# Transposing bf16 data as fp32 pairs in a channel-attention and mixture-of-adapters kernel

## The chip, the cores and the metric

The kernel runs on one core of a Trainium2 chip. The metric is the device time of one execution in microseconds. The kernel before takes 255.24 us (median of 2 runs, 255.1 to 255.38). Its profile covers a span of 253.5 us.

## The reference

For each of four batches, q and k (6400 rows by 256 channels) are normalised along the rows. Their 256 by 256 channel product goes through a softmax, and v is multiplied by it. On each row of the result, a gate picks two of eight experts by its logits; each expert is a rank-16 adapter, and its output is added to the row.

```python
qn = q / (np.linalg.norm(q, axis=1, keepdims=True) + 1e-06)
kn = k / (np.linalg.norm(k, axis=1, keepdims=True) + 1e-06)
a = softmax(kn.transpose(0, 2, 1) @ qn / tau)          # 256 x 256, per batch
x = v @ a                                              # 25600 x 256
# logits = x @ w_gate; two largest of 8 -> weights w
# out = x + sum over the two experts e of  w_e * (x @ A[e]) @ B[e]
```

## The kernel before

A planner orders all steps ahead of time and fixes the engine of each. Four steps matter here. `do_G` builds the channel product on TensorE with k as the stationary operand. `do_T` transposes v on TensorE, 128 x 128 bf16 at a time, into PSUM; `do_Te` copies the result to SBUF on ScalarE or VectorE ("eviction"). The gated product `gz` is formed on VectorE, transposed on TensorE (`do_gzT`) and evicted. `do_Y` multiplies the transposed v by the softmax and the transposed gated product by the adapters' B. Between them, matmuls with the transposed v as weights give logits and adapter inputs (`do_ZL`, `do_log`, `do_Z`).

```python
# cut: constants P = 128, CC = 2 channel halves, C = 256, E = 8, ER = 128; a unit u has n = 4 or 2 columns
    def do_G(s, b, c):
        if c == 0:
            st[b]["acc"] = [psum.tile([P, 512], FP32, tag=f"acc{ic}", name=f"acc{ic}") for ic in range(CC)]
        acc = st[b]["acc"]
        (qt, j), (kt, _) = qk_of("q", b, c), qk_of("k", b, c)
        for ic in range(CC):
            nc.tensor.matmul(
                acc[ic][:, 0:256], kt[:, j, ic * P:(ic + 1) * P], qt[:, j, :],
                start=c == 0, stop=False, skip_group_check=True)
# cut: k against itself and q against itself, for the norms:
        for ic in range(0 if (b, group_of(c), "k") in OFF else CC):
            nc.tensor.matmul(
                acc[ic][:, 256:384], kt[:, j, ic * P:(ic + 1) * P],
                kt[:, j, ic * P:(ic + 1) * P],
                start=False, stop=False, skip_group_check=True)
# cut
    def do_T(s, b, i, u):
        c, n = UNITS[u]
        g = max(g for g, (i0, _) in enumerate(V) if i0 <= i)
        vt = held["v", (b, g), ""][:, (i - V[g][0]) * PC:, :]
        sb(s, "vT", (b, i), [P, CC, PC, P], BF16)
        ps = bank(s, ("T", b, i, u), [P, CC, n, P], BF16)
        for ic in range(CC):
            for j in range(n):
                nc.tensor.matmul(
                    ps[:, ic, j, :], vt[:, c + j, ic * P:(ic + 1) * P], W["ident"],
                    is_transpose=True, start=(ic + j == 0), stop=(ic == CC - 1 and j == n - 1))

    def do_Te(s, b, i, u):
        c, n = UNITS[u]
        copy(s, held["vT", (b, i), ""][:, :, c:c + n, :], held["bank", ("T", b, i, u)])
# cut
    def do_Ze(s, b, i, u):
        c, n = UNITS[u]
        gz = sb(s, "gz", (b, i, u), [P, n, ER], BF16)
        z = held["zl", (b, i), ""][:, c:c + n, E:] if (b, i) in MERGED else held["bank", ("Z", b, i, u)]
        nc.vector.tensor_tensor(
            out=gz.rearrange("p c (e r) -> p c e r", e=E),
            in0=z.rearrange("p c (e r) -> p c e r", e=E),
            in1=held["gate", (b, i), "g2"][:, c:c + n, :].to_broadcast([P, n, E, R]), op=OP.mult)
# cut
    def do_gzT(s, b, i, u):
        c, n = UNITS[u]
        gz = held["gz", (b, i, u), ""]
        sb(s, "gzT", (b, i, u), [P, n, P], BF16)
        ps = bank(s, ("gzT", b, i, u), [P, n, P], BF16)
        for j in range(n):
            nc.tensor.matmul(ps[:, j, :], gz[:, j, :], W["ident"], is_transpose=True,
                             start=(j == 0), stop=(j == n - 1))
# cut
    def do_Y(s, b, i, c):
        u = unit_of(c)
        vT, gzT = held["vT", (b, i), ""], held["gzT", (b, i, u), ""]
        ps = bank(s, ("Y", b, i, c), [P, 2, C], FP32)
        for j in range(2):
            for ic in range(CC):
                nc.tensor.matmul(
                    ps[:, j, :], vT[:, ic, c + j, :], st[b]["a"][:, ic, :],
                    start=(j == 0 and ic == 0), stop=False, skip_group_check=True)
        for j in range(2):
            nc.tensor.matmul(ps[:, j, :], gzT[:, c + j - UNITS[u][0], :], W["B"],
                             start=False, stop=(j == 1), skip_group_check=True)
```

## Time and profile before

| | before |
|---|---|
| time, median | 255.24 us |
| busy TensorE / VectorE / ScalarE | 215.6 / 190.1 / 167.6 us |
| bf16 transposes of v and of gz | 400 and 200 |
| HBM read and written | 78.9 and 26.2 MB, 415 GB/s over the span |
| last TensorE matmul, last eviction, end of span | 245.4, 246.0, 253.5 us |

These lines are from the profile's page of the kernel before: busy time of each engine, then the granted TensorE clock and the busy share of the DMA engines in tenths over 40 slices, then groups of instructions. A group shows line, engine and operation, tile written and read, shapes and count, then busy us and the mean ns of one instruction, then idle time before it and who ended that.

```profile
PE 215.6 (85%) x2643; PEld 192.3 (76%) x2643; DVE 190.1 (75%) x486; ACT 167.6 (66%) x270; POOL 29.9 (12%) x58
...
PEclk9999897699999999999999999999999999999996
DMA  9999999999999999999999999999999999999994
...
L750 ACT COPY vT<-T_ps 128x1024 bf16<-128x1024 bf16 (+1 forms) x44 | 37.0, 871 | 6.7 <-PE T_ps L770 6.5
...
L770 PE MATMUL T_ps<-ident,v 128*128 128x128 bf16 x400 | 26.8, 219 | 0.8 <-DMA v<-in_v_dram 0.8
...
L870 DVE TENSOR_TENSOR gz<-zl,gateg 128x512 bf16<-128x512 f32 (+1 forms) x42 | 23.5, 597 | 0.3
...
L881 PE MATMUL gzT_ps<-ident,gz 128*128 128x128 bf16 x200 | 19.7, 219 | 0.3
```

DMA is busy for nine tenths or more of nearly every slice. A bf16 transpose has a record of 219 ns, but the records overlap, so that is a latency (from start to end of one) and not a cost (the time for which it keeps the engine from the next). The cost is read from the chain of waits, which gives start, length and count of each piece of a stream:

```profile
137.56 0.44 PE Y_ps L894 x4
137.99 0.22 PE Y_ps L898 x2
138.21 1.12 PE T_ps L770 x20
139.33 0.22 PE acc L575 x2
139.54 0.11 PE acc L579 x2
```

Twenty transposes take 1.12 us: 56 ns each. Two 256-column matmuls take 0.22 us (109 ns each) and two 128-column ones 0.11 us (56 ns).

The last view before the change gives busy us in stretches of the span: columns as in the header, then the granted clock, the DMA share and GB/s.

```profile
core 0: us, PE busy (x) PEld busy (x) DVE busy (x) ACT busy (x) POOL busy (x), PEclk, DMA share, GB/s
230.00:240.00 10.00, 10.00 (x132) 9.27 (x131) 8.66 (x25) 7.82 (x15) 0.00 (x0) 1.00 1.01 423
244.00:246.00 2.00, 1.40 (x13) 1.01 (x11) 0.00 (x0) 1.79 (x4) 0.00 (x0) 1.00 1.00 408
246.00:248.00 2.00, 0.00 (x0) 0.00 (x0) 0.00 (x0) 0.02 (x1) 0.00 (x0) 1.00 1.02 414
248.00:250.00 2.00, 0.00 (x0) 0.00 (x0) 0.00 (x0) 0.00 (x0) 0.00 (x0) 0.92 0.74 297
```

### The profile page before, as it was taken

How to read it: one execution, taken by the hardware profiler on the slowest of the kernel's cores; microseconds unless marked ns; L12 is line 12 of the kernel's file. 1: busy time of each engine (PE TensorE's matmuls, PEld its weight loads, DVE VectorE, ACT ScalarE, POOL GpSimd, SP SyncE). 2: the span in 40 equal slices, each digit the busy share in tenths (PEclk: the TensorE clock that was granted, in tenths of full speed). 3: DMA queues.
4: the chain of work that ended last, by engine and by line, in shares of the span. 5: the costliest groups of instructions: out<-in, count | busy, mean ns of one | idle time of the engine just before them, and what ended most of it. 6: DMA issues, size and time to landing. Idle time of an engine off the chain costs nothing.

```text
span 253.5 us, 6344 instructions
## 1 busy us (share of the span) xinstructions
PE 215.6 (85%) x2643; PEld 192.3 (76%) x2643; DVE 190.1 (75%) x486; ACT 167.6 (66%) x270; POOL 29.9 (12%) x58
## 2 busy tenths in 40 slices
PE   1173993899999999999989999979999979999970
PEld 0051982688999996799779999779999869989860
DVE  0055589779889978898979995689888888888910
ACT  4354437558786767888758768453877869768770
POOL 7001220040020002000030100510000210000000
PEclk9999897699999999999999999999999999999996
DMA  9999999999999999999999999999999999999994
GB/s 223 211 215 212 212 217 213 213 216 216 218 215 211 318 295 293 259 214 219 209 216 221 217 216 217 210 211 345 284 278 323 331 322 319 316 421 427 427 411 196
DMA packets 11820, 66.60 MB, mean 263 GB/s; under 512 B 1424, under 2 KB 2320, under 8 KB 7184
## 3 DMA queue, kind: packets, MB, share of 16 engines
q0 software_dynamic: 7488, 38.93, 74.8%
q1 hardware_dynamic: 3968, 26.74, 26.0%
q10 hardware_dynamic: 336, 0.53, 0.6%
q8 instruction: 20, 0.33, 0.5%
q14 instruction: 8, 0.07, 0.1%
HBM read 78.91 MB, written 26.21 MB: 415 GB/s over the span
## 4 chain that ended last, share of the span: by engine, by line
PE 49%; DMA 39%; ACT 3%; DVE 3%; POOL 2%; issue 1%; ACTq 0%; POOLq 0%
DMA qk<-in_k_dram 22%; PE Y_ps L894 13%; DMA v<-in_v_dram 9%; DMA qk<-in_q_dram 8%; PE acc L575 7%; PE Y_ps L898 6%; PE T_ps L770 6%; PE ZL_ps L792 4%; PE gzT_ps L881 3%; PE acc L584 2%; PE acc L579 2%; PE Z_ps L861 2%; DVE a_bf L744 2%; ACT a_exp L696 1%; PE log_ps L807 1%
## 5 line engine op out<-in xcount | busy, mean ns | idle before, releaser
L575 PE MATMUL acc<-qk 128*128 128x256 bf16 x400 | 70.6, 286 | 20.1 <-DMA qk<-in_k_dram 14.0
L603 DVE TENSOR_TENSOR ssq<-ssq,sq 128x1280 f32<-128x1280 f32 (+1 forms) x27 | 43.4, 1607 | 26.8 <-ACT sq L597 24.8
L894 PE MATMUL Y_ps<-a_bf,vT 128*128 128x256 bf16 x400 | 60.0, 273 | 0.0
L597 ACT ACTIVATE sq<-qk 128x1280 f32<-128x1280 bf16 (+1 forms) x27 | 36.8, 1364 | 26.2 <-DVE ssq L603 19.7
L750 ACT COPY y<-Y_ps 128x512 f32<-128x512 f32 x79 | 45.7, 587 | 12.4 <-PE Y_ps L898 9.8
L575 PEld LDWEIGHTS <-qk 128*128 128x128 bf16 x400 | 33.7, 102 | 24.4 <-DMA qk<-in_k_dram 16.0
L750 ACT COPY vT<-T_ps 128x1024 bf16<-128x1024 bf16 (+1 forms) x44 | 37.0, 871 | 6.7 <-PE T_ps L770 6.5
L894 PEld LDWEIGHTS <-vT 128*128 128x128 bf16 x400 | 37.6, 98 | 3.7
L898 PE MATMUL Y_ps<-ball,gzT 128*128 128x256 bf16 x200 | 38.2, 273 | 0.3 <-DVE gzT L752 0.3
L579 PE MATMUL acc<-qk 128*128 128x128 bf16 x242 | 34.0, 223 | 0.0
L770 PE MATMUL T_ps<-ident,v 128*128 128x128 bf16 x400 | 26.8, 219 | 0.8 <-DMA v<-in_v_dram 0.8
L560 POOL DMA_DIRECT2D v<-in_v_dram x20 | 12.2, 609 | 126.9 <-PE T_ps L770 80.7
L579 PEld LDWEIGHTS <-qk 128*128 128x128 bf16 x242 | 24.4, 101 | 3.5
L770 PEld LDWEIGHTS <-v 128*128 128x128 bf16 x400 | 23.7, 98 | 1.7 <-DMA v<-in_v_dram 1.4
L870 DVE TENSOR_TENSOR gz<-zl,gateg 128x512 bf16<-128x512 f32 (+1 forms) x42 | 23.5, 597 | 0.3
L584 PE MATMUL acc<-qk 128*128 128x128 bf16 x168 | 23.5, 222 | 0.0
L898 PEld LDWEIGHTS <-gzT 128*128 128x128 bf16 x200 | 19.4, 98 | 3.0 <-DVE gzT L752 0.6
L792 PE MATMUL ZL_ps<-waA_sb,vT 128*128 128x136 bf16 x280 | 19.6, 222 | 1.1 <-DVE waA_sb L738 0.9
L881 PE MATMUL gzT_ps<-ident,gz 128*128 128x128 bf16 x200 | 19.7, 219 | 0.3
L752 DVE COPY gzT<-gzT_ps 128x512 bf16<-128x512 bf16 (+1 forms) x39 | 15.0, 390 | 5.6 <-PE gzT_ps L881 4.8
L792 PEld LDWEIGHTS <-vT 128*128 128x128 bf16 x280 | 17.7, 98 | 1.8 <-issue 1.5
L597 ACT ACTIVATE ssq<-qk 128x1536 f32<-128x1536 bf16 x8 | 11.9, 1483 | 9.7 <-DMA qk<-in_q_dram 5.1
(79 smaller groups left out, 273.8 us busy)
## 6 DMA issues: line engine op xcount, KB each, us to landing
out_dram<-y SPq DMA_DIRECT2D x18, 1280.0 KB, 17.9
v<-in_v_dram POOLq DMA_DIRECT2D x20, 640.0 KB, 20.5
qk<-in_q_dram POOLq DMA_DIRECT2D x7, 1088.0 KB, 24.1
qk<-in_k_dram POOLq DMA_DIRECT2D x7, 1088.0 KB, 28.8
qk<-in_q_dram POOLq DMA_DIRECT2D x2, 1024.0 KB, 18.7
qk<-in_k_dram POOLq DMA_DIRECT2D x2, 1024.0 KB, 23.1
out_dram<-y SPq DMA_DIRECT2D x4, 512.0 KB, 7.0
qk<-in_q_dram POOLq DMA_DIRECT2D x2, 512.0 KB, 17.1
```

Of the source, the lines that this page charges most:

```text
L575: nc.tensor.matmul(acc[ic][:, 0:256], kt[:, j, ic * P:(ic + 1) * P], qt[:, j, :], start=c == 0, stop=False, skip_group_check=True)
L579: nc.tensor.matmul(acc[ic][:, 256:384], kt[:, j, ic * P:(ic + 1) * P], kt[:, j, ic * P:(ic + 1) * P], start=False, stop=False, skip_group_ ...
L584: nc.tensor.matmul(acc[ic][:, 384:512], qt[:, j, ic * P:(ic + 1) * P], qt[:, j, ic * P:(ic + 1) * P], start=False, stop=c == NC - 1, skip_ ...
L597: nc.scalar.activation(out[:, 0:n, :], t[:, j:j + n, :], ACT.Square)
L603: nc.vector.tensor_tensor(out=t, in0=t, in1=held["sq", (w, b, g), ""][:, 0:n, :], op=OP.add)
L750: nc.scalar.copy(out, in_)
L770: nc.tensor.matmul(ps[:, ic, j, :], vt[:, c + j, ic * P:(ic + 1) * P], W["ident"], is_transpose=True, start=(ic + j == 0), stop=(ic == CC ...
L792: nc.tensor.matmul(ps[:, j, :], vT[:, ic, c + j, :], st[b]["waA"][:, ic, :], start=(j == 0 and ic == 0), stop=(j == n - 1 and ic == CC - 1 ...
L870: nc.vector.tensor_tensor(out=gz.rearrange("p c (e r) -> p c e r", e=E), in0=z.rearrange("p c (e r) -> p c e r", e=E), in1=held["gate", (b ...
L881: nc.tensor.matmul(ps[:, j, :], gz[:, j, :], W["ident"], is_transpose=True, start=(j == 0), stop=(j == n - 1))
L894: nc.tensor.matmul(ps[:, j, :], vT[:, ic, c + j, :], st[b]["a"][:, ic, :], start=(j == 0 and ic == 0), stop=False, skip_group_check=True)
L898: nc.tensor.matmul(ps[:, j, :], gzT[:, c + j - UNITS[u][0], :], W["B"], start=False, stop=(j == 1), skip_group_check=True)
```

## The change

The intent is to halve the transposes. Two neighbouring bf16 values are taken as one fp32 value, so that one 128 x 128 fp32 transpose moves what two bf16 transposes moved. After it, each partition holds a pair of even and odd channel, so the weights taken from the transposed v are read at every second bf16, and k's channels are taken with stride 2 to match. For the gated product the pair is two neighbouring rows. VectorE must therefore write gz interleaved, which it does with one instruction for every two columns in place of one for the unit.

```diff
         ident = const.tile([P, P], BF16, name="ident")
         make_identity(nc, ident)
         W["ident"] = ident
+        W["ident32"] = const.tile([P, P], FP32, name="ident32")
+        nc.vector.tensor_copy(W["ident32"], ident)
 # cut; the channel product, k with stride 2 (also in the row-norm sums of k):
             nc.tensor.matmul(
-                acc[ic][:, 0:256], kt[:, j, ic * P:(ic + 1) * P], qt[:, j, :],
+                acc[ic][:, 0:256], kt[:, j, ic::CC], qt[:, j, :],
                 start=c == 0, stop=False, skip_group_check=True)
         for ic in range(0 if (b, group_of(c), "k") in OFF else CC):
             nc.tensor.matmul(
-                acc[ic][:, 256:384], kt[:, j, ic * P:(ic + 1) * P],
-                kt[:, j, ic * P:(ic + 1) * P],
+                acc[ic][:, 256:384], kt[:, j, ic::CC],
+                kt[:, j, ic::CC],
                 start=False, stop=False, skip_group_check=True)
         for ic in range(0 if (b, group_of(c), "q") in OFF else CC):
             nc.tensor.matmul(
 # cut; transposes of v, and how their result is read:
-        sb(s, "vT", (b, i), [P, CC, PC, P], BF16)
-        ps = bank(s, ("T", b, i, u), [P, CC, n, P], BF16)
-        for ic in range(CC):
-            for j in range(n):
-                nc.tensor.matmul(
-                    ps[:, ic, j, :], vt[:, c + j, ic * P:(ic + 1) * P], W["ident"],
-                    is_transpose=True, start=(ic + j == 0), stop=(ic == CC - 1 and j == n - 1))
+        sb(s, "vT", (b, i), [P, PC, P], FP32)
+        ps = bank(s, ("T", b, i, u), [P, n, P], FP32)
+        for j in range(n):
+            nc.tensor.matmul(ps[:, j, :], vt[:, c + j, :].bitcast(FP32), W["ident32"],
+                             is_transpose=True, start=(j == 0), stop=(j == n - 1))
 
     def do_Te(s, b, i, u):
         c, n = UNITS[u]
-        copy(s, held["vT", (b, i), ""][:, :, c:c + n, :], held["bank", ("T", b, i, u)])
+        copy(s, held["vT", (b, i), ""][:, c:c + n, :], held["bank", ("T", b, i, u)])
+
+    def vT_of(b, i, c):
+
+        return held["vT", (b, i), ""][:, c, :].bitcast(BF16).rearrange("p (t cc) -> p t cc", cc=CC)
 # cut; the same in do_log and do_Z:
-                    ps[:, j, :], vT[:, ic, c + j, :], st[b]["waA"][:, ic, :],
+                    ps[:, j, :], vT_of(b, i, c + j)[:, :, ic], st[b]["waA"][:, ic, :],
 # cut; the gated product and its transposes:
-        nc.vector.tensor_tensor(
-            out=gz.rearrange("p c (e r) -> p c e r", e=E),
-            in0=z.rearrange("p c (e r) -> p c e r", e=E),
-            in1=held["gate", (b, i), "g2"][:, c:c + n, :].to_broadcast([P, n, E, R]), op=OP.mult)
+        pairs = gz.rearrange("p c d -> p (c d)").rearrange("p (h x two) -> p h two x", two=2, x=ER)
+        for h in range(n // 2):
+            nc.vector.tensor_tensor(
+                out=pairs[:, h].rearrange("p c (e r) -> p c e r", e=E),
+                in0=z[:, 2 * h:2 * h + 2, :].rearrange("p c (e r) -> p c e r", e=E),
+                in1=held["gate", (b, i), "g2"][:, c + 2 * h:c + 2 * h + 2, :].to_broadcast([P, 2, E, R]), op=OP.mult)
 
     def do_gzT(s, b, i, u):
         c, n = UNITS[u]
         gz = held["gz", (b, i, u), ""]
-        sb(s, "gzT", (b, i, u), [P, n, P], BF16)
-        ps = bank(s, ("gzT", b, i, u), [P, n, P], BF16)
-        for j in range(n):
-            nc.tensor.matmul(ps[:, j, :], gz[:, j, :], W["ident"], is_transpose=True,
-                             start=(j == 0), stop=(j == n - 1))
+        sb(s, "gzT", (b, i, u), [P, n // 2, P], FP32)
+        ps = bank(s, ("gzT", b, i, u), [P, n // 2, P], FP32)
+        pairs = gz.rearrange("p c d -> p (c d)").bitcast(FP32)
+        for j in range(n // 2):
+            nc.tensor.matmul(ps[:, j, :], pairs[:, j * P:(j + 1) * P], W["ident32"], is_transpose=True,
+                             start=(j == 0), stop=(j == n // 2 - 1))
 # cut; do_Y:
-                    ps[:, j, :], vT[:, ic, c + j, :], st[b]["a"][:, ic, :],
+                    ps[:, j, :], vT_of(b, i, c + j)[:, :, ic], st[b]["a"][:, ic, :],
                     start=(j == 0 and ic == 0), stop=False, skip_group_check=True)
         for j in range(2):
-            nc.tensor.matmul(ps[:, j, :], gzT[:, c + j - UNITS[u][0], :], W["B"],
+            pair = gzT[:, (c - UNITS[u][0]) // 2, :].bitcast(BF16).rearrange("p (t two) -> p t two", two=2)
+            nc.tensor.matmul(ps[:, j, :], pair[:, :, j], W["B"],
                              start=False, stop=(j == 1), skip_group_check=True)
 
```

The tile of zeros for warm-up matmuls is halved and read twice, to make room for the fp32 identity.

More of the change, by code (lines that the diff above doesn't have):

```diff
@@ L507, in make_consts @@
         W["neg"] = neg
-        W["zeros"] = const.tile([P, 512], BF16, name="zeros")
+        W["zeros"] = const.tile([P, 256], BF16, name="zeros")
         nc.vector.memset(W["zeros"], 0.0)
@@ L616, in do_n2p @@
         for ic in range(CC):
-            nc.tensor.matmul(ps[:, ic:ic + 1], st[b]["ssq" + w][:, ic * P:(ic + 1) * P],
+            half = slice(ic, None, CC) if w == "k" else slice(ic * P, (ic + 1) * P)
+            nc.tensor.matmul(ps[:, ic:ic + 1], st[b]["ssq" + w][:, half],
                              W["ones"][:, 0:1], start=(ic == 0), stop=(ic == CC - 1),
@@ L757, in do_warm @@
     def do_warm(s, n):
-        nc.tensor.matmul(bank(s, ("warm", n), [P, 512], FP32), W["ident"], W["zeros"],
+        nc.tensor.matmul(bank(s, ("warm", n), [P, 512], FP32), W["ident"], W["zeros"][:, None, :].to_broadcast([P, 2, 256]),
                          start=True, stop=True)
@@ L786, in do_ZL @@
         c, n = ZUNITS[z]
-        vT = held["vT", (b, i), ""]
         sb(s, "zl", (b, i), [P, PC, E + ER], FP32)
@@ L801, in do_log @@
     def do_log(s, b, i):
-        vT = held["vT", (b, i), ""]
         gate_tiles(s, b, i)
@@ L807, in do_log @@
                 nc.tensor.matmul(
-                    ps[:, j, :], vT[:, ic, j, :], st[b]["awg"][:, ic, :],
+                    ps[:, j, :], vT_of(b, i, j)[:, :, ic], st[b]["awg"][:, ic, :],
                     start=(j == 0 and ic == 0), stop=(j == PC - 1 and ic == CC - 1),
@@ L855, in do_Z @@
         c, n = UNITS[u]
-        vT = held["vT", (b, i), ""]
         sb(s, "gz", (b, i, u), [P, n, ER], BF16)
@@ L861, in do_Z @@
                 nc.tensor.matmul(
-                    ps[:, j, :], vT[:, ic, c + j, :], st[b]["aA"][:, ic, :],
+                    ps[:, j, :], vT_of(b, i, c + j)[:, :, ic], st[b]["aA"][:, ic, :],
                     start=(j == 0 and ic == 0), stop=(j == n - 1 and ic == CC - 1),
@@ L889, in do_Y @@
         u = unit_of(c)
-        vT, gzT = held["vT", (b, i), ""], held["gzT", (b, i, u), ""]
+        gzT = held["gzT", (b, i, u), ""]
         ps = bank(s, ("Y", b, i, c), [P, 2, C], FP32)
```

## The prediction

> **What bounds it now.** Two things at once. The page's slices show DMA at 9 tenths in all but the last; HBM moves 415 GB/s; the windows view has a DMA share of 0.95 to 1.08 in every 10 us up to 250. That traffic is untouched. From about 52 us on TensorE is full too: 9.4 to 10.0 us busy per 10 us nearly everywhere, and the chain of waits is TensorE without a break from 208 to 245 us, then one eviction and the last store (to 253.5). VectorE is busy 75%, ScalarE 66%.
>
> **What the change does.**
>
> 1. TensorE, transposes: 400 + 200 bf16 become 200 + 100 fp32. A bf16 one costs 56 ns in a stream (20 in 1.12 us in the chain), a pair 112. No fp32 transpose is in the trace. Its fp32 matmuls: with one column, four records take 0.42 us, so an fp32 weight load takes about 105 ns, against at most 24 to 28 for bf16 (8-column logit matmuls); with 256 columns a pass takes about 240 ns, double the bf16 109. The Trainium skill, "TensorE: Matmul & The Clock Gate", Weight-path perf modes, says fast weight load needs a non-FP32 dtype; the trace agrees. Every fp32 instruction here leaves two records (two passes), but the page's Terms call transpose mode 4x faster for FP32, which I take as one pass; no run shows it. Then an fp32 transpose is bound by its weight load, 105 to 120 ns (estimate), equal to the pair it replaces: 300 x (-7 to +8 ns) = -2 to +2 us. With two passes, 210 to 240 ns: +30 to +38 us.
> 2. TensorE, stride 2: k weights, moving k, and all weights from vT and gzT read every second bf16. "SBUF — State Buffer", cachelines note: stride is free up to 8 bf16. No instruction of before shows it; I expect intervals of 109, 59 and 56 ns unchanged. Without fast load, 128- and 136-column matmuls would go from 56-59 to about 105 ns.
> 3. ScalarE: vT evictions 1015 to about 590 ns (29), 593 to 385 (15), gzT 585 to 385 (12): -19 us busy.
> 4. VectorE: its bf16 evictions were already fast (684 ns for 1024 bf16, 690 for 512 fp32): no gain. The gate product splits: 40 of 687 ns become 80 of about 416, +6 us busy, and each transpose starts 0.15 us later.
>
> The order of steps on each engine stays; transposes merge.
>
> **On the critical path.** ScalarE's 19 us are not (late in the span it waits mostly for TensorE). Of VectorE's 6 us perhaps 1. The TensorE terms are, from 52 us on, and cancel to within 2 us. The DMA floor forbids much gain: a TensorE saving of 15 us would show 2 to 4.
>
> **Predicted: 256.0 us, range 252.5 to 277.** Faster by over 2%: 0.03; within 2%: 0.66; slower by over 2%: 0.31. The high side carries two passes and lost fast load.
>
> **What would show it.** 200 and 100 transpose records, ten in about 1.1 us (twice the records or 2 us: step 1 wrong). Intervals of Y 109, merged logit 59, k Gram 56 ns: step 2 right. ScalarE busy near 149 us, VectorE near 196. DMA at 9 tenths throughout, last y eviction at 245 to 247 us.
>
> **What would make it wrong.** Two passes; transpose-mode loads that cannot be prefetched behind a running matmul; strided weights without fast load (+20 us or more); fp32 transposes that let the granted clock fall below 1.0 after 60 us; VectorE, near 0.9 busy in mid-span, pushed over by the split product.

## More of the kernel before

The timeline shows two transposes of gz between 256-column matmuls of Y, with TensorE's weight loads (PEld) beside them. Columns are start, length, engine and instruction:

```profile
239.22 0.21 PEld L881 LDWEIGHTS <-gz 128*128 128x128 bf16 x2
239.33 0.28 PE L881 MATMUL gzT_ps<-ident,gz 128*128 128x128 bf16 x2
...
239.44 0.38 PE L894 MATMUL Y_ps<-a_bf,vT 128*128 128x256 bf16 x2
```

From the start of the first transpose (239.33) to the start of the next matmul (239.44) TensorE gives 0.11 us to the pair.

TensorE looks full from 230 to 240 us, with DMA full beside it. After TensorE has ended, DMA goes on at 414 GB/s for two more microseconds and is not idle before 250.

## The result, and the profile after

| | before | after |
|---|---|---|
| time, median of 2 runs | 255.24 us | 255.25 us (255.21 to 255.28) |
| busy TensorE / VectorE / ScalarE | 215.6 / 190.1 / 167.6 | 218.9 / 193.2 / 150.0 us |
| transposes of v and of gz | 400 and 200 bf16 | 200 and 100 fp32 |
| span | 253.5 us | 253.4 us |

The ratio is 0.9995, 95% interval 0.9971 to 1.0019: the same. Ratios with an interval are not quite the ratio of the quoted medians.

The page after, the same groups:

```profile
PE 218.9 (86%) x2343; PEld 193.1 (76%) x2343; DVE 193.2 (76%) x527; ACT 150.0 (59%) x270; POOL 29.9 (12%) x58
...
PEclk9999996599999999999999999999999999999996
DMA  8999999999999999999999999999999999999995
...
L772 PE MATMUL T_ps<-ident,v 128*128 128x128 f32 x200 | 27.8, 281 | 0.6 <-DMA v<-in_v_dram 0.6
...
L753 ACT COPY vT<-T_ps 128x512 f32<-128x512 f32 (+1 forms) x44 | 21.7, 516 | 9.2 <-PE T_ps L772 8.8
...
L874 DVE TENSOR_TENSOR gz<-zl,gateg 128x256 bf16<-128x256 f32 x70 | 26.0, 444 | 0.3
...
L886 PE MATMUL gzT_ps<-ident,gz 128*128 128x128 f32 x100 | 20.4, 278 | 0.0
```

There is one record for each fp32 transpose, 200 and 100, and not two. ScalarE's evictions of v fell from 37.0 to 21.7 us. VectorE's largest group of gz rose from 23.5 to 26.0 us; that line leaves out the products read straight from PSUM, which went from 10.6 to 11.4 us. TensorE's busy time rose by 3.3 us although the intervals below show no more work: it counts all time covered by a record, and a record (281 and 278 ns for an fp32 transpose) lasts longer than the engine is held. The intervals in the chain of waits say what was paid:

```profile
137.41 0.11 PE Y_ps L904
137.52 1.09 PE T_ps L772 x10
138.61 0.22 PE acc L577 x2
138.83 0.11 PE acc L581 x2
```

Ten fp32 transposes take 1.09 us, 109 ns each, for what took 112 ns as two bf16 ones. The channel product, now with k at stride 2 both as weights (L577) and as the moving operand (L581), still takes 0.22 and 0.11 us for two. The timeline around one lone fp32 transpose of gz:

```profile
239.21 0.38 PE L904 MATMUL Y_ps<-ball,gzT 128*128 128x256 bf16 x2
...
239.32 0.14 PEld L886 LDWEIGHTS gzT_ps<-ident,gz 128*128 128x128 f32 x1
239.42 0.27 PE L886 MATMUL gzT_ps<-ident,gz 128*128 128x128 f32 x1
239.43 0.21 PEld L899 LDWEIGHTS <-vT 128*128 128x128 bf16 x2
239.53 0.27 PE L899 MATMUL Y_ps<-a_bf,vT 128*128 128x256 bf16 x1
```

Its weight load starts at 239.32, while the matmuls of B are still running, and the transpose still holds TensorE from 239.42 to 239.53: 0.11 us, as the pair of bf16 ones did at the same place. The last stretches:

```profile
core 0: us, PE busy (x) PEld busy (x) DVE busy (x) ACT busy (x) POOL busy (x), PEclk, DMA share, GB/s
230.00:240.00 10.00, 10.00 (x112) 9.29 (x111) 8.97 (x30) 6.99 (x15) 0.00 (x0) 1.00 1.01 425
244.00:246.00 2.00, 1.48 (x14) 1.08 (x11) 0.00 (x0) 1.79 (x4) 0.00 (x0) 1.00 1.01 413
246.00:248.00 2.00, 0.00 (x0) 0.00 (x0) 0.00 (x0) 0.11 (x1) 0.00 (x0) 1.00 1.03 415
248.00:250.00 2.00, 0.00 (x0) 0.00 (x0) 0.00 (x0) 0.00 (x0) 0.00 (x0) 0.67 0.77 309
```

DMA has the same shares in the same places.

### The profile page after: what moved, and what is told of

Read it like the earlier page. It is cut to its first block, busy times and chain, and to the rows that moved or that the text cites. A ratio compares the mean times of both kernels' runs of the same rounds, so it can differ in the third digit from the quotient of the medians.

```text
span 253.4 us, 5843 instructions
## 1 busy us (share of the span) xinstructions
PE 218.9 (86%) x2343; PEld 193.1 (76%) x2343; DVE 193.2 (76%) x527; ACT 150.0 (59%) x270; POOL 29.9 (12%) x58
## 4 chain that ended last, share of the span: by engine, by line
PE 49%; DMA 42%; DVE 2%; ACT 2%; POOL 1%; issue 1%; ACTq 0%; POOLq 0%
DMA qk<-in_k_dram 28%; PE Y_ps L899 12%; PE acc L577 9%; DMA qk<-in_q_dram 8%; PE T_ps L772 6%; PE Y_ps L904 6%; DMA v<-in_v_dram 6%; PE ZL_ps L796 4%; PE gzT_ps L886 4%; PE acc L586 2%; PE acc L581 2%; PE Z_ps L863 2%; PE log_ps L810 1%; DVE a_bf L747 1%; POOL qk L562 1%
## 5 line engine op out<-in xcount | busy, mean ns | idle before, releaser
L577 PE MATMUL acc<-qk 128*128 128x256 bf16 x400 | 71.2, 285 | 17.5 <-DMA qk<-in_k_dram 10.7
L577 PEld LDWEIGHTS <-qk 128*128 128x128 bf16 x400 | 34.7, 103 | 22.7 <-DMA qk<-in_k_dram 13.6
L899 PEld LDWEIGHTS <-vT 128*128 128x128 bf16 x400 | 38.9, 98 | 4.0
L581 PE MATMUL acc<-qk 128*128 128x128 bf16 x242 | 34.4, 224 | 0.0
L772 PE MATMUL T_ps<-ident,v 128*128 128x128 f32 x200 | 27.8, 281 | 0.6 <-DMA v<-in_v_dram 0.6
L753 ACT COPY vT<-T_ps 128x512 f32<-128x512 f32 (+1 forms) x44 | 21.7, 516 | 9.2 <-PE T_ps L772 8.8
L581 PEld LDWEIGHTS <-qk 128*128 128x128 bf16 x242 | 24.3, 100 | 3.4
L874 DVE TENSOR_TENSOR gz<-zl,gateg 128x256 bf16<-128x256 f32 x70 | 26.0, 444 | 0.3
L772 PEld LDWEIGHTS T_ps<-ident,v 128*128 128x128 f32 x200 | 23.0, 145 | 1.8 <-DVE gatemsum L842 0.7
L886 PE MATMUL gzT_ps<-ident,gz 128*128 128x128 f32 x100 | 20.4, 278 | 0.0
L796 PEld LDWEIGHTS <-vT 128*128 128x128 bf16 x280 | 17.8, 98 | 1.9 <-issue 1.5
L755 DVE COPY gzT<-gzT_ps 128x256 f32<-128x256 f32 (+1 forms) x39 | 14.9, 390 | 4.2 <-PE gzT_ps L886 3.6
```

Of the source, the lines that this page charges most:

```text
L577: nc.tensor.matmul(acc[ic][:, 0:256], kt[:, j, ic::CC], qt[:, j, :], start=c == 0, stop=False, skip_group_check=True)
L581: nc.tensor.matmul(acc[ic][:, 256:384], kt[:, j, ic::CC], kt[:, j, ic::CC], start=False, stop=False, skip_group_check=True)
L753: nc.scalar.copy(out, in_)
L772: nc.tensor.matmul(ps[:, j, :], vt[:, c + j, :].bitcast(FP32), W["ident32"], is_transpose=True, start=(j == 0), stop=(j == n - 1))
L796: nc.tensor.matmul(ps[:, j, :], vT_of(b, i, c + j)[:, :, ic], st[b]["waA"][:, ic, :], start=(j == 0 and ic == 0), stop=(j == n - 1 and ic ...
L874: nc.vector.tensor_tensor(out=pairs[:, h].rearrange("p c (e r) -> p c e r", e=E), in0=z[:, 2 * h:2 * h + 2, :].rearrange("p c (e r) -> p c ...
```

## The experiments

The first theory was: an fp32 transpose costs TensorE what its two bf16 ones cost, and the changes on ScalarE and VectorE are off the critical path. The rivals: a gain from ScalarE cancels against a loss from the split product on VectorE (rival 2); or the DMA floor hides whatever TensorE does, and equal time says nothing (rival 3). Twelve kernels ran, four on one chip at a time.

### One part at a time

**a1: only v in pairs, the gated product as before.**

```diff
 # after, with the old do_Ze, do_gzT and B matmul:
-        sb(s, "gzT", (b, i, u), [P, n // 2, P], FP32)
+        sb(s, "gzT", (b, i, u), [P, n, P], BF16)
 # cut
```

> The change with v transposed as pairs but the gated product left as before (bf16 transposes, one product instruction). It keeps about 15 us of ScalarE's saving and drops the 6 us that the split product adds on VectorE. Theory 1 (an fp32 transpose costs what its two bf16 ones cost, and the savings and costs of ScalarE and VectorE are off the critical path): 255.2 us, within 0.4% of before. Rival 2 (a real gain from ScalarE's evictions is cancelled by a real loss from the split product): 1 to 2% faster than before, about 251 to 253 us.

Measured: correct, 255.49 us against 255.61 of before on the same chip, ratio 0.9993 (0.998 to 1.0006). ScalarE was busy 152.6 us, VectorE 190.0.

**a2: only the gated product in pairs, v and k as before.**

```diff
 # before, with the new do_Ze, do_gzT and B matmul:
-        sb(s, "gzT", (b, i, u), [P, n, P], BF16)
+        sb(s, "gzT", (b, i, u), [P, n // 2, P], FP32)
 # cut
```

> The other part alone: the gated product split and transposed as pairs, v and k as before. ScalarE saves about 3 us, VectorE pays about 8. Theory 1: 255.2 us, within 0.4% of before. Rival 2: 0.8 to 2% slower, about 257 to 260 us.

Measured: correct, 255.83 us, ratio 1.0009 (0.9994 to 1.0023). VectorE busy 193.0 us.

**a3: the kernel before, evicting the same bytes as fp32.**

```diff
-        copy(s, held["vT", (b, i), ""][:, :, c:c + n, :], held["bank", ("T", b, i, u)])
+        copy(s, held["vT", (b, i), ""][:, :, c:c + n, :].bitcast(FP32), held["bank", ("T", b, i, u)].bitcast(FP32))
 # cut; the same in do_gzTe
```

> The kernel before with its bf16 transposes, but the copies out of PSUM read and write the same bytes as half as many fp32 elements: ScalarE's saving (about 17 us busy) with nothing else of the change. Correct result expected. Theory 1: 255.2 us, within 0.4%. Rival 2: 251 to 253 us. In the profile ScalarE busy about 150 us, VectorE about 190, 600 bf16 transposes at 56 ns.

Measured: correct, 255.49 us, ratio 0.9997 (0.9981 to 1.0012). ScalarE fell to 150.1 us, so this edit of two lines has the whole of the change's saving on ScalarE without touching a transpose. It bought no time.

**a4: the kernel before with the split product only.**

```diff
-        nc.vector.tensor_tensor(
-            out=gz.rearrange("p c (e r) -> p c e r", e=E),
+        for h in range(n // 2):
+            nc.vector.tensor_tensor(
+                out=gz[:, 2 * h:2 * h + 2, :].rearrange("p c (e r) -> p c e r", e=E),
 # cut; in0 and in1 sliced alike
```

> The kernel before with only the gated product split into one instruction for every two rows, plain layout. VectorE pays 6 to 8 us busy, nothing is saved. Theory 1: 255.2 us, within 0.4%. Rival 2: 257 to 260 us.

Measured: correct, 255.49 us, ratio 0.9995 (0.9981 to 1.0008). VectorE busy 192.6 us. Its group of products, from the profile's groups of this run, which writes gz without interleaving:

```profile
L871 DVE TENSOR_TENSOR gz<-zl,gateg 128x256 bf16<-128x256 f32 x70 | 25.4, 418 | 0.3
```

One costs 418 ns here and 444 ns in the changed kernel, where the bf16 output has stride 2.

None of the four moves the time by more than 0.1%, and every interval holds 1. Rival 2 needed a gain in a1 and a3 of 1% or more and a loss in a2 and a4; it falls. That says what the parts are worth in this kernel, not what they would cost without a floor.

### How far TensorE can move

**b3: each fp32 transpose issued twice.**

```diff
         for j in range(n):
-            nc.tensor.matmul(ps[:, j, :], vt[:, c + j, :].bitcast(FP32), W["ident32"],
-                             is_transpose=True, start=(j == 0), stop=(j == n - 1))
+            for x in range(2):
+                nc.tensor.matmul(ps[:, j, :], vt[:, c + j, :].bitcast(FP32), W["ident32"],
+                                 is_transpose=True, start=(j + x == 0), stop=(j == n - 1 and x == 1))
 # cut; the same in do_gzT
```

> The changed kernel with each of its 300 fp32 transposes issued twice (result unchanged, still correct): TensorE gets 300 x 109 ns = 33 us of work, nearly all after 52 us, and nothing else changes. Theory 1 with TensorE on the critical path from about 52 us on: some 5 us of it fill TensorE's waits and warm-up matmuls, the rest shows: 277 to 286 us. Rival 3 (the DMA floor decides and hides what TensorE does, so equal time says nothing of the cost of a transpose): under 260 us.

Measured: 278.69 us, ratio 1.0908 (1.0881 to 1.0935), but the result was wrong (relative error inf). The second transpose of a tile did not start its bank anew, and its output was probably added to the first; d1, which starts the bank anew, is correct.

**d1: the same, mended; each group is run twice in full.**

```diff
-        for j in range(n):
+        for j in list(range(n)) * 2:
             nc.tensor.matmul(ps[:, j, :], vt[:, c + j, :].bitcast(FP32), W["ident32"],
 # cut; the same in do_gzT
```

> The earlier doubled-transpose kernel mended: each group of fp32 transposes is run twice over in full, the second time starting its bank anew, so the result should be correct now. 33 us more TensorE work. The earlier one measured 278.7 us with a wrong result. All theories: 277 to 280 us if the wrong values did not change the timing.

Measured: correct, 278.47 us, ratio 1.0914 (1.0892 to 1.0935).

**d2: the kernel before with its bf16 transposes doubled in the same way.**

```diff
-        for ic in range(CC):
+        for ic in list(range(CC)) * 2:
             for j in range(n):
 # cut; the same in do_gzT over j
```

> The kernel before with each group of its bf16 transposes run twice: 600 x 56 ns = 33.6 us more TensorE work. Theory 1 (an fp32 transpose costs its pair of bf16 ones, 109 against 112 ns): the same as the doubled fp32 kernel within 1%, 277 to 282 us. If fp32 transposes were really cheaper or dearer by 20 ns each and the floor hid it: 6 us apart or more.

Measured: correct, 279.73 us, ratio 1.0953 (1.093 to 1.0976). So 300 fp32 transposes (300 x 109 ns = 32.7 us) add 23.1 us to 255.38 of before on that chip, and 600 bf16 ones (600 x 56 = 33.6 us) add 24.4. The difference, 1.3 us, has the sign of the difference of the costs (0.9 us), but the two intervals overlap, so it is not shown to be more than noise. With the work doubled, the two forms give the same time within half a per cent. In the chains of waits of d1 and d2 no DMA is left after 52 us, and the page of d1 shows that TensorE is pushed past DMA, which now has slices of four to seven tenths:

```profile
DMA  9999999999999999994569999899999999974476
```

It also shows slack: about 10 us of the 33 did not reach the time.

**b4: one B matmul of each pair left out.**

```diff
-        for j in range(2):
+        for j in range(1, 2):
             pair = gzT[:, (c - UNITS[u][0]) // 2, :].bitcast(BF16).rearrange("p (t two) -> p t two", two=2)
```

> The changed kernel with one of the two 256-column matmuls of the gated product in each output pair left out (wrong result on purpose): TensorE loses 100 x 109 ns = 11 us, 10 of them after 60 us; DMA, ScalarE and VectorE keep all their work. If TensorE alone bounds: about 245 us. If the DMA floor stands close below (what I predicted: a saving of 15 us shows as 2 to 4): 252.5 to 254.

Measured: 255.64 us against 255.66 of before, ratio 1.0 (0.9977 to 1.0024). The kernel leaves out half of the adapters' output and is wrong by construction, yet the comparison with the reference passed, presumably because that output is small beside v @ a. So "correct" does not vouch for the gated product and its transposes. Eleven microseconds less on TensorE gave nothing. The same stretches of the span in this run:

```profile
core 0: us, PE busy (x) PEld busy (x) DVE busy (x) ACT busy (x) POOL busy (x), PEclk, DMA share, GB/s
230.00:240.00 10.00, 10.00 (x111) 9.20 (x110) 9.68 (x32) 7.62 (x18) 0.00 (x0) 1.00 1.01 423
244.00:246.00 2.00, 0.00 (x0) 0.00 (x0) 0.00 (x0) 0.20 (x1) 0.00 (x0) 1.00 0.97 389
246.00:248.00 2.00, 0.00 (x0) 0.00 (x0) 0.00 (x0) 0.00 (x0) 0.00 (x0) 0.55 1.02 414
248.00:250.00 2.00, 0.00 (x0) 0.00 (x0) 0.00 (x0) 0.00 (x0) 0.00 (x0) 0.50 0.78 315
```

TensorE has nothing left to do in 244 to 246 us, where both kernels still had 1.4 to 1.5 us of it, and DMA is as full as ever up to 248 us. The last results are ready earlier, the last store is issued at 244.2 us instead of 246.1 (after), and the span is no shorter. But TensorE ends only 1.9 us earlier (243.57 against 245.48) for 11 us of work less: the rest turned into waits, those for k's loads going from 10.7 us to 15.2. The chain of waits moved to DMA, first in the kernel after, then in b4:

```profile
PE 49%; DMA 42%; DVE 2%; ACT 2%; POOL 1%; issue 1%; ACTq 0%; POOLq 0%
DMA 61%; PE 26%; issue 4%; POOL 2%; DVE 2%; ACT 2%; POOLq 0%; ACTq 0%
```

**c1: 8 of 10 columns stored in the whole-tile stores (output incomplete).**

```diff
+        n = {10: 8}.get(n, n)
         nc.sync.dma_start(out_v[b, :, lo:lo + n, :], held["y", (b, i), ""][:, c:c + n, :])
```

> The changed kernel storing 8 of 10 columns in each whole-tile store (18 of 20 tiles; output incomplete on purpose): 4.7 MB of 105 MB less traffic, about 11 us of DMA time at 415 GB/s, no compute removed. If DMA alone bounds: about 244 us. If TensorE bounds from 52 us on: 251 to 255 us.

Measured: 249.62 us, ratio 0.9767 (0.9736 to 0.9798): 6.0 us less. Neither forecast holds alone; DMA bounds for the first 6 of 11 us, then something else does.

**c2: b4 and c1 together.**

```diff
-        for j in range(2):
+        for j in range(1, 2):
 # and
+        n = {10: 8}.get(n, n)
```

> Both of the last two: 11 us less on TensorE and 11 us less DMA. If the two limits stand side by side, this gives clearly more than the sum of the two alone: 244 to 248 us. If only one of them bounds, it gives what that one alone gives.

Measured: 246.36 us, ratio 0.9642 (0.9614 to 0.9671): 9.3 us less, where the two alone give 0.0 and 6.0. The same matmuls that were worth nothing under full stores are worth 3.3 us once the stores are cut. So DMA is the first limit in the changed kernel and TensorE the second, some 6 us below it. The kernel before was not run with b4's edit; e1 below shows that fewer stores shorten it too.

### Before against after with the first limit out of the way

If DMA is the first limit, equal times of before and after could hide a difference of compute. So both kernels were run with only 4 of 10 columns stored.

**e1 (before) and e2 (after).**

```diff
+        n = {10: 4}.get(n, n)
         nc.sync.dma_start(out_v[b, :, lo:lo + n, :], held["y", (b, i), ""][:, c:c + n, :])
```

> The kernel before storing 4 of 10 columns in its whole-tile stores (output incomplete on purpose): 14 MB less traffic, about 34 us of DMA time, so that the DMA floor is out of the way of compute. Expected 244 to 250 us, bound by TensorE and the loads that feed it. It is the baseline for its partner, the changed kernel with the same stores.

> The changed kernel with the same 4 of 10 columns stored. Theory 1 (the costs are equal on TensorE and the rest is off the path even without the floor): within 0.6% of its partner, either sign (TensorE estimate -2 to +2 us). Rival 3 (the floor hid a real difference): over 1% apart from its partner: faster if the saved ScalarE time or cheaper transposes were worth something, slower if the split product or the strided reads cost something.

Measured: e1 248.33 us (248.1 to 248.5), e2 248.73 us (248.43 to 248.83). The two medians are 0.16% apart (248.73 / 248.33). The outputs are incomplete. Stretches of e1, with the columns of the header:

```profile
core 0: us, PE busy (x) PEld busy (x) DVE busy (x) ACT busy (x) POOL busy (x), PEclk, DMA share, GB/s
...
220.00:230.00 10.00, 10.00 (x138) 9.21 (x136) 8.79 (x29) 7.25 (x13) 0.00 (x0) 1.00 0.27 107
...
242.00:244.00 2.00, 0.40 (x4) 0.11 (x2) 0.00 (x0) 0.96 (x2) 0.00 (x0) 1.00 1.00 395
```

The same stretches of e2:

```profile
core 0: us, PE busy (x) PEld busy (x) DVE busy (x) ACT busy (x) POOL busy (x), PEclk, DMA share, GB/s
...
220.00:230.00 10.00, 10.00 (x118) 9.23 (x116) 8.99 (x32) 6.39 (x13) 0.00 (x0) 1.00 0.27 107
...
242.00:244.00 2.00, 0.84 (x8) 0.50 (x6) 0.00 (x0) 1.32 (x3) 0.00 (x0) 1.00 0.83 328
```

From 220 to 230 us TensorE is full and DMA at 0.27: compute bounds here. Up to 210 us, though, the loads still keep DMA at a share of 0.97 to 1.06 in both runs, so fewer stores did not empty it there. The chain of waits is the evidence for that part: in e1 and e2 it holds DMA only before 52 us (19% of the span). TensorE ends 0.4 us later in e2 (0.84 us busy after 242 against 0.40). This is the whole visible difference, and it is against the change, not for it. Rival 3 said more than 1%; in the form "the floor hides a real difference" it falls. Its other half, that the floor would hide what TensorE does, is true for work taken away: b4 shows it.

## Why the prediction was right

The predicted 256.0 us and "within 2%" held (255.25). Point by point:

- **Step 1, transposes on TensorE: right.** One record each, ten in 1.09 us, so 109 ns against the estimated 105 to 120. The saving of TensorE time is 300 x (112 - 109) = 0.9 us, inside the forecast of -2 to +2. Doubling both kinds (d1, d2) agrees in elapsed time. The reason given, the weight load, is not shown: the load of the lone transpose starts at 239.32, but its record of 0.14 us ends after the transpose has begun at 239.42, so either the load or the streaming of 128 fp32 columns can be what takes 0.11 us. No run separates the two.
- **Step 2, stride 2: right.** Intervals stayed at 109 ns (Y, channel product), 59 (merged logits, twenty in 1.18 us in both kernels) and 56 ns (k against itself). The Trainium skill, "SBUF — State Buffer", cachelines note, allows eight bf16 within a 16-byte line; reads by TensorE at two agree (larger steps were not run).
- **Step 3, ScalarE: right.** -17.6 us against -19, and worth nothing (a3).
- **Step 4, VectorE: direction right, size not.** +3.1 us busy against +6. Two adjacent products overlap: in the timeline after 239.3 us two of them took 0.78 us together, where 2 x 444 ns would be 0.89 and one undivided product took 0.68.
- **The critical path: this step failed.** The prediction said that TensorE is full from 52 us on, that its terms are on the critical path, and that a saving of 15 us would show 2 to 4. For added work this held in part: of 33 us, about 23 showed (d1). For work taken away it failed: a saving of 11 us showed 0.0 (b4). Windows with 10.0 of 10 us busy and an unbroken chain of TensorE pieces at the end had been read as a limit. The chain names one sequence without a gap; it does not say that shortening it would help, since the stores behind it were queued anyway. And the same chain of the kernel before has two long loads after 52 us, which the prediction passed over:

```profile
98.10 29.72 DMA qk<-in_k_dram
141.40 20.85 DMA qk<-in_q_dram
```

  The failed step did no harm to the number, because the TensorE terms cancelled. That is luck in part: with DMA as the first limit, a saving of 11 us would have given the same time. The Trainium skill, "Trainium Kernel Development and Optimization", Performance Expectations, warns that matmul busy time is a bad metric because matmuls are pipelined. This agrees: 218.9 us busy after against 215.6 before, at no more work.
- **The DMA floor: right, and stronger than said.** Removing 4.7 MB of stores gave 6.0 us at once.

What stays open: the 0.4 us between e1 and e2. VectorE's 0.1 us longer product per unit is an unlikely cause. In the two chains of waits e2 is 0.24 us behind at the merged logits of 65 us, 0.41 at those of 77, and 0.44 behind both at 206 us (Y from 205.79 against 206.23) and at the last eviction (242.44 against 242.88). Over those last 36 us (one profile each), with 30 fp32 transposes of v and 30 of gz from 208 us on, nothing was lost or won.

No version here beats both kernels with a complete output. The way down is less DMA time, and by fewer stores alone it is worth only about 7 us (e1), after which compute bounds.

## What to carry to other kernels

Packing two bf16 values into an fp32 transpose halves the instructions but did not halve TensorE's time here: the fp32 one took twice as long (109 against 56 ns). If only the eviction is to be cheaper, reading and writing the same bf16 bytes as fp32 does that alone. When two resources look full, subtract work from each in turn and from both: here a cut that helped only the second limit showed nothing until the first had been moved (b4, c1, c2). To learn what a change costs under a floor, compare both kernels with the floor lowered, and with the changed work doubled.

## What the Trainium skill lacked or had wrong

- "TensorE: Matmul & The Clock Gate", Terms, calls transpose mode "4× faster for FP32"; it gives no time and does not say faster than what. Here 128 fp32 columns took 109 ns in transpose mode, 0.85 ns a column. An fp32 matmul of 256 columns left two records and held TensorE for 0.49 us (198.00 to 198.49 us in the kernel before; 0.43 in the kernel after, 197.62 to 198.05), 1.7 to 1.9 ns a column. Against that it is about 2 times, not 4; no fp32 matmul of 128 columns was run.
- The same page, Part 4, gives 275 to 390 ns for a 128 x 128 bf16 transpose. Records here are 219 ns long, but a stream costs 56 ns each, which the page does not give. It also says that the full clock does not engage for transposes; with every fp32 transpose doubled (d1) the granted clock was 1.00 in every stretch from 100 to 270 us. Those transposes stand between matmuls; none ran alone here.
- "PSUM — Partial Sum Buffer" says that 1- and 2-byte transposes never accumulate and that an fp32 one sets the written bits. It does not warn of a second fp32 transpose onto the first without a new start, though its rule of adding where those bits are set would explain it: relative error inf in b3, correct in d1.
- No page found gives VectorE's cost of a bf16 output at stride 2: 444 ns against 418 for a 256-element product (after against a4).
